# One due time in a fused attention and expert kernel: the turns of a tile are emitted ahead of the next scores

## Chip, cores and metric

The kernel runs on one core of a Trainium2 chip. The time is the device time of one execution in microseconds (us); lower is better. TensorE is called PE, VectorE DVE, ScalarE ACT, GpSimd POOL and SyncE SP, as the profile calls them.

## The reference

Three stages follow each other: attention with a rotation of q and k, a dense layer pair with a gate, and a layer of 8 experts of which each token takes one.

```python
q_rot, k_rot = (rotate(q), rotate(k))            # batch 2, heads 8, seq 576, head_dim 64
scores = scale * np.matmul(q_rot, k_rot.transpose(0, 1, 3, 2))
scores = scores - np.max(scores, axis=-1, keepdims=True)
attn = np.exp(scores)
attn = attn / (np.sum(attn, axis=-1, keepdims=True) + 1e-09)
attn_out = np.matmul(attn, v)
x = attn_out.transpose(0, 2, 1, 3).reshape(B * S, H * D)   # 1152 x 512
h = x @ w_in                                     # 512 x 2048
x = (h * (1.0 / (1.0 + np.exp(-1.702 * h)))) @ w_out
...
expert_idx = np.argmax(x @ w_gate, axis=1)       # 8 experts, at most capacity tokens each
y = np.maximum(disp @ w1, 0.0) @ w2              # per expert, 512 x 1024 x 512
out[i] = gate_w[i] * y[expert_idx[i], pos[i]]
```

## The kernel before, in words

Attention (class `Attention`) goes over 8 pairs p of heads. The queries of a pair stand in 9 tiles i of 128 rows (tile 4 holds the left-over rows of both heads). For each tile:

- `scores(p, i)` (L370) multiplies on PE into a PSUM tile `s` (L393, four matmuls, ten for tile 4), and DVE takes the negated row maximum `nm` from it (L397). `s` has two buffers (pool `ps_s`), so scores i waits until the exponential of scores i-2 has read its buffer.
- `exps(p, i)` (L400) is ACT's exponential of `s` into `pp`, with row sums (L404).
- `turn(p, i)` (L427) transposes the exponentials on PE, four transposes into a PSUM tile `tp` (L442; L434 for tile 4), and copies it to `pt` on ACT or DVE (L212 on ACT, L214 on DVE; the table `SWAPPED` says which).

Around these stand, for each pair: `turn_rest` (tile `tr`, L452), which turns the last 64 columns, and its copies to `ptr`; `turn_sums` (tile `trb`, L472), which turns the reciprocals `rr` of the row sums, and its copy to `tb`; `pv_units` (tile `pv`, L493), the product with v for the two halves a of the pair's tokens, whose last unit multiplies by `tb` on DVE (L496) and writes `xt`; and `qk_units` (tile `tq`, L329), which turns the rotated q and k of the next pair and copies them to `qs` and `ks`. The last q copy is followed by two SP transfers of `qs` into `qx` with the halves exchanged (L344, L345), which the scores of the next pair read. All of `tp`, `tr`, `trb`, `pv` and `tq` come from one PSUM pool of four buffers, `ps_t`.

The order is made in two steps. `run` (L507) gives every unit a due time, one time unit per tile and nine per pair, sorts by it and emits in that order:

```python
at = 9 * p
for i in range(9):
    add(max(at + i - 2 + ORDER["scores"], -1), self.scores, p, i)   # L524
    add(max(at + i - 2 + ORDER["exps"], -1), self.exps, p, i)
    add(at + i + ORDER["turn"], self.turn, p, i)                    # L526
for a in range(2):
    add(at + 4 + 4 * a + ORDER["rest"][a], self.turn_rest, p, a)
    add(at + 4 + 4 * a + ORDER["sums"][a], self.turn_sums, p, a)    # L529
...
    add(at - 9 + ORDER["qk"][k], part, self.qk_units, p, k)         # L536
```

So `scores(p, i+3)` is due at 9p+i+0.174 and `turn(p, i)` at 9p+i+0.191. Then the tile framework, at build time (`TC` at L42 asks it to plan with a model of the machine), lays out the instructions of each engine: among those it holds ready it takes the one emitted first. The order on an engine therefore is not the order of emission: a unit that is not ready is passed by others. On the chip each engine then runs its list in that order.

After attention the class `Experts` computes the dense pair (`first`, `ffn`, `hidden`: L686 and L712), routes the tokens (`route`) and runs the experts (`second`, `few`).

Of the kernel before, what the change touches and what calls it, by code (L numbers as in the profile page):

```python
# [88 lines left out]
WIDE = max(b - a for a, b in zip(CUTS, CUTS[1:])) * TT  # L89
ORDER = {  # L90
    "scores": -0.826,
    "turn": 0.191,
    "exps": 0.692,
    "pv1": (-0.327, 1.359, 1.489, 1.566, 3.949),
    "split": (-0.927, -0.14, 0.12, 2.55),
# [1013 lines left out]
```

## Time and profile before

| What | Value |
|---|---|
| Median of three runs | 508.85 us (507.22 to 508.88) |
| The profiled execution's own time | 510.11 us |
| Its span from the first to the last instruction | 508.3 us |
| PE matmul busy over the span | 469.7 us (92%) |
| DVE, ACT, POOL busy over the span | 366.7 us, 271.6 us, 115.0 us |
| Mean granted TensorE clock | 0.983 |

Busy time is the share of time in which an engine has an instruction under way. Matmuls are pipelined and their ends are modelled, so PE's busy time counts some overlap. A time in brackets behind a row is idle time of the engine ahead of it, with the instruction that ended the wait.

### The profile page before, as it was taken

To read this page: it belongs to the slowest core of one execution; us is meant where nothing else is said; L and a number is where in the kernel's file an instruction comes from. 1 tells how busy PE (TensorE), PEld (TensorE's weight loads), DVE (VectorE), ACT (ScalarE), POOL (GpSimd) and SP (SyncE) were. 2 spreads that over 40 slices of the span, in tenths; PEclk is the share of its full clock that TensorE was granted. 3 is DMA by queue.
4 is the path that set the end of the run, shared out by engine and by line. 5 is a ranking of instruction groups with operands and counts; after the bars stand their busy time and mean duration, and the time that the engine had idled before them with its cause. 6 is when DMAs were issued, how large, how long until landed. Compare 5 with 4: busy or idle time off the path is not lost.

```text
span 508.3 us, 8728 instructions
## 1 busy us (share of the span) xinstructions
PE 469.7 (92%) x3206; PEld 421.6 (83%) x3206; DVE 366.7 (72%) x746; ACT 271.6 (53%) x514; POOL 115.0 (23%) x117
## 2 busy tenths in 40 slices
PE   1789999998999999999999999999999999499992
PEld 1777687687787778788899999999999999499991
DVE  6798999888788998999835534457856689355570
ACT  3577686676565733534563444466566455254640
POOL 5965633422211200000000000000444025601020
PEclk9999999999999999999999999999999999699997
DMA  7032322330224357574101240001076436735410
GB/s 256 1 100 75 99 77 74 99 80 26 53 64 155 105 187 254 188 265 177 41 1 31 63 170 1 0 11 55 2 250 206 132 125 195 246 97 191 162 50 14
DMA packets 20125, 55.63 MB, mean 109 GB/s; under 512 B 3685, under 2 KB 4869, under 8 KB 20080
## 3 DMA queue, kind: packets, MB, share of 16 engines
q1 hardware_dynamic: 17920, 50.91, 31.3%
q0 software_dynamic: 1728, 3.62, 2.4%
q8 instruction: 27, 0.44, 0.4%
q10 hardware_dynamic: 432, 0.51, 0.3%
q14 instruction: 18, 0.15, 0.1%
HBM read 43.86 MB, written 6.66 MB: 99 GB/s over the span
## 4 chain that ended last, share of the span: by engine, by line
PE 61%; DVE 16%; DMA 10%; issue 5%; ACT 4%; POOL 1%; SPq 0%; POOLq 0%; DVEq 0%; ACTq 0%
PE h L686 22%; PE y L712 20%; PE s L393 6%; PE pv L493 4%; DMA qx<-qs 3%; PE tp L442 3%; DVE nm L397 2%; DMA raw<-in_w_out 2%; PE tr L758 2%; DMA raw<-in_w_in 2%; DVE hl L298 2%; ACT pp L404 1%; DVE m L588 1%; DMA got<-x,ent 1%; POOL slots L868 1%
## 5 line engine op out<-in xcount | busy, mean ns | idle before, releaser
L686 PE MATMUL h<-xt,hl 128*128 128x288 f32 (+4 forms) x960 | 175.2, 322 | 1.2 <-DVE hl L673 1.2
L686 PEld LDWEIGHTS h<-xt,hl 128*128 128x128 f32 x960 | 149.0, 191 | 10.2 <-DVE hl L673 2.8
L673 DVE TENSOR_TENSOR hl<-wf,hl 128x1024 fp32r<-128x1024 f32 x80 | 97.5, 1223 | 53.6 <-ACT hl L672 53.4
L712 PE MATMUL y<-gh,hl 128*128 128x288 f32 (+3 forms) x576 | 126.0, 324 | 0.0
L672 ACT ACTIVATE hl<-wf 128x1024 fp32r<-128x1024 f32 x80 | 84.3, 1058 | 52.5 <-PE y L712 25.5
L712 PEld LDWEIGHTS y<-gh,hl 128*128 128x128 f32 x576 | 96.2, 190 | 3.9 <-ACT gh L722 0.4
L712 PE MATMUL y<-gl,hl 128*128 128x288 f32 (+3 forms) x288 | 78.1, 321 | 0.0
L868 POOL DMA_INDIRECT slots<-entry,r_at x12 | 16.5, 1375 | 207.6 <-ACT hl L672 176.8
L397 DVE TENSOR_REDUCE nm<-s 128x1 f32<-128x576 f32 x72 | 53.8, 752 | 12.3 <-PE s L393 10.9
L404 ACT ACTIVATE pp<-s,nm 128x576 f32<-128x576 f32 x64 | 47.7, 745 | 22.7 <-DVE nm L397 22.4
L721 ACT ACTIVATE g<-h 128x480 f32<-128x480 f32 (+2 forms) x48 | 23.5, 492 | 62.6 <-PE h L686 53.2
L393 PE MATMUL s<-ks,qs 128*128 128x288 f32 (+1 forms) x168 | 53.0, 333 | 1.7 <-ACT pp L404 1.3
L712 PEld LDWEIGHTS y<-gl,hl 128*128 128x128 f32 x288 | 51.2, 188 | 1.8
L393 PE MATMUL s<-ks,qx 128*128 128x288 f32 (+1 forms) x168 | 47.0, 306 | 3.4 <-DMA qx<-qs 2.6
L723 DVE TENSOR_TENSOR gl<-g,gh 128x480 fp32r<-128x480 f32 (+2 forms) x48 | 26.5, 554 | 25.1 <-ACT gh L722 24.3
L212 ACT ACTIVATE pt<-tp 128x512 f32<-128x512 f32 x56 | 33.3, 600 | 20.5 <-PE tp L442 20.0
L442 PE MATMUL tp<-ident,pp 128*128 128x128 f32 x256 | 39.8, 281 | 0.5 <-DVE ptr L214 0.5
L493 PE MATMUL pv<-pt,vr 128*64 128x288 f32 x256 | 39.1, 414 | 0.5 <-DVE pt L214 0.3
L393 PEld LDWEIGHTS s<-ks,qs 128*128 128x128 f32 x168 | 32.7, 196 | 7.8 <-issue 3.5
L393 PEld LDWEIGHTS s<-ks,qx 128*128 128x128 f32 x168 | 32.9, 197 | 4.8 <-issue 2.0
L442 PEld LDWEIGHTS tp<-ident,pp 128*128 128x128 f32 x256 | 30.5, 143 | 5.3 <-issue 2.6
L329 PE MATMUL tq<-ident_r,hl 128*128 128x128 f32 x144 | 18.7, 264 | 14.1 <-DVE hl L298 13.5
(178 smaller groups left out, 580.4 us busy)
## 6 DMA issues: line engine op xcount, KB each, us to landing
wf<-in_w SPq DMA_DIRECT2D x32, 512.0 KB, 4.1
raw<-in_w_in SPq DMA_DIRECT2D x16, 512.0 KB, 4.0
raw<-in_w_out SPq DMA_DIRECT2D x16, 512.0 KB, 4.0
qx<-qs SPq DMA_DIRECT2D x14, 320.0 KB, 4.3
qk<-in_qk SPq DMA_DIRECT2D x12, 288.0 KB, 3.2
vr<-in_v SPq DMA_DIRECT2D x8, 320.0 KB, 5.6
x<-row SPq DMA_DIRECT2D x12, 192.0 KB, 2.1
out<-zero SPq DMA_DIRECT2D x9, 256.0 KB, 3.0
```

What stands on the lines that cost most here:

```text
L212: return e.activation(out=out, in_=x, func=AF.Copy, **({} if scale is None else {"scale": scale}))
L393: nc.tensor.matmul(ps[:, n, c:c + w], x, ks[:, src:src + w], start=j == 0, stop=j == len(mine) - 1)
L397: nc.vector.tensor_reduce(out=nm, in_=ps[:, :, 0:HALF], axis=AX.XY, op=ALU.max, negate=True)
L404: nc.scalar.activation(out=out.rearrange("p (n k) -> p n k", n=2), in_=ps[:, :, 0:HALF], func=AF.Exp, bias=d["nm"][:, i:i + 1], accum_out= ...
L442: nc.tensor.transpose(t[:, kt], pp[:, h, h * 64 + kt * P:h * 64 + (kt + 1) * P], self.ident)
L493: nc.tensor.matmul(o[h * 64:h * 64 + 64], x, y, start=j < 2, stop=j > 7)
L672: nc.scalar.activation(out=hl[:, 0], in_=t, func=AF.Copy)
L673: self.last = nc.vector.tensor_tensor(out=hl[:, 1], in0=t, in1=hl[:, 0].bitcast(F32), op=ALU.subtract).ins
L686: self.nc.tensor.matmul(h, u, v, start=m == 0, stop=m == len(ops) - 1)
L712: nc.tensor.matmul(y[j][:, 0:w], u, v, start=f == LAG and m == 0, stop=f == n + LAG - 1 and m == 2)
L721: nc.scalar.activation(out=g, in_=h, func=AF.Gelu_apprx_sigmoid)
L723: nc.vector.tensor_tensor(out=gl, in0=g, in1=gh.bitcast(F32), op=ALU.subtract)
```

## The change

One number in the table of due times is made smaller, so that `turn(p, i)` is due at 9p+i+0.160, ahead of `scores(p, i+3)` at 9p+i+0.174.

```diff
 ORDER = {
     "scores": -0.826,
-    "turn": 0.191,
+    "turn": 0.16,
     "exps": 0.692,
```

Two other units have due times between 0.160 and 0.191 of a step, and the turn now goes ahead of them as well: `turn_sums(p-1, 1)`, due at 9p+0.187, which stood ahead of `turn(p, 0)`; and the first `qk_units` of the next pair (the function `rest` at L350, two transposes and two copies), due at 9p+3.185, which stood ahead of `turn(p, 3)`. No instruction is added or taken away.

## Rows read from the trace of the kernel before

**Rows 1.** Busy time by stretch (PE, PEld, DVE, ACT, POOL; granted clock third from last)

```profile
16.00:185.00 169.00, 161.52 (x1191) 127.76 (x1191) 149.39 (x292) 112.97 (x261) 65.03 (x67) 1.00 0.29 83
...
220.00:300.00 80.00, 79.83 (x423) 73.45 (x422) 52.55 (x93) 37.01 (x54) 0.00 (x0) 1.00 0.29 101
```

**Rows 2.** Waits of PE from 15 to 185 us: total, times, longest

```profile
PE s L393 <- DMA qx<-qs: 2.6, 4, 1.3
```

**Rows 3.** Timeline of PE, first and last turn with the scores behind

```profile
20.52 1.05 PE L442 MATMUL tp<-ident,pp 128*128 128x128 f32 x4
21.23 0.61 PE L393 MATMUL s<-ks,qs 128*128 128x288 f32 x1
...
165.92 0.60 PE L442 MATMUL tp<-ident,pp 128*128 128x128 f32 x4
166.94 0.40 PE L393 MATMUL s<-ks,qs 128*128 128x288 f32 x1 [0.42 <-ACT pp L404]
```

**Rows 4.** Groups of DVE from 15 to 185 us: the turns that DVE copies

```profile
L214 DVE COPY pt<-tp 128x512 f32<-128x512 f32 x16 | 10.8, 677 | 0.0
```

**Rows 5.** Timeline of PE around the start of pair 3

```profile
79.89 0.40 PE L393 MATMUL s<-ks,qs 128*128 128x288 f32 x1 [0.89 <-ACT pp L404]
...
80.62 0.71 PE L493 MATMUL pv<-ptr,vr 128*64 128x288 f32 x4
...
81.25 0.44 PE L472 MATMUL trb<-ident,rr 128*128 128x128 f32 x2
...
81.53 0.60 PE L442 MATMUL tp<-ident,pp 128*128 128x128 f32 x4
```

**Rows 6.** Timeline of PE where pairs 1, 4 and 5 begin

```profile
39.55 0.41 PE L472 MATMUL trb<-ident,rr 128*128 128x128 f32 x2 [0.46 <-DVE rr L214]
...
98.31 0.44 PE L442 MATMUL tp<-ident,pp 128*128 128x128 f32 x2 [0.54 <-DVE ptr L214]
...
119.19 0.44 PE L472 MATMUL trb<-ident,rr 128*128 128x128 f32 x2
119.54 0.40 PE L393 MATMUL s<-ks,qs 128*128 128x288 f32 x1
```

**Rows 7.** Timeline of ACT: the exponential that the last scores of rows 6 wait for

```profile
118.66 0.74 ACT L404 ACTIVATE pp<-s,nm 128x576 f32<-128x576 f32 x1 [3.43 <-DVE nm L397]
```

**Rows 8.** Timeline of PE in pair 2: the next pair's transposes and turn 3

```profile
65.61 0.36 PE L329 MATMUL tq<-ident_r,hl 128*128 128x128 f32 x2
65.81 0.37 PE L393 MATMUL s<-ks,qs 128*128 128x288 f32 x1
...
66.42 0.60 PE L442 MATMUL tp<-ident,pp 128*128 128x128 f32 x4
66.77 0.88 PE L329 MATMUL tq<-ident_r,hl 128*128 128x128 f32 x8
```

**Rows 9.** Timeline of DVE at the same place of pair 1

```profile
46.90 0.28 DVE L214 CAST qs<-tq 128x128 fp32r<-128x128 f32 x1
47.10 0.28 DVE L216 TENSOR_SCALAR ks<-tq 128x128 fp32r<-128x128 f32 x1
47.44 0.76 DVE L397 TENSOR_REDUCE nm<-s 128x1 f32<-128x576 f32 x1
...
49.56 0.71 DVE L397 TENSOR_REDUCE nm<-s 128x1 f32<-128x576 f32 x1
```

**Rows 10.** Timeline of PE: the longest wait for the exchanged q

```profile
115.92 0.37 PE L393 MATMUL s<-ks,qx 128*128 128x288 f32 x1 [1.33 <-DMA qx<-qs]
```

**Rows 11.** Timeline of PE among the experts, ahead of and behind a long wait

```profile
431.73 1.28 PE L686 MATMUL h<-xt,hl 128*128 128x224 f32 x10
...
441.18 0.87 PE L963 MATMUL tg<-ident,got 96*128 96x96 f32 x4 [6.60 <-DMA got<-x,ent]
441.75 2.46 PE L686 MATMUL h<-xt,hl 128*128 128x224 f32 x10
```

**Rows 12.** Busy time by stretch, as rows 1, behind that wait

```profile
442.00:444.00 2.00, 2.00 (x11) 2.00 (x11) 0.56 (x1) 0.49 (x1) 0.00 (x0) 0.50 0.74 213
```

## The prediction

> **What bounds the kernel now.** I first read the busy time by stretch, to see which stage the change can reach. Attention runs to about 185 us, and in its 169 us from 16 us on PE has work under way for 161.5 us, DVE for 149.4 us and ACT for 113.0 us; in the dense pair behind it PE has no gap to speak of, 79.83 of 80 us [rows 1]. So what attention gains or loses is handed on to the end nearly whole, and in attention itself no more than 169 - 161.5 = 7.5 us of PE's idle time could be had. Then I read PE's waits there: the largest that comes back in the loop is the one for the exchanged q, 2.6 us in four places [rows 2]. A step of the change is worth something only if it alters such a wait, or PE's work in front of it.
>
> Then I read PE's timeline unit by unit, and this is the reading that decides. The change swaps turn i and scores i+3 in the order of emission. On PE they already stand in the new order. The first turn runs at 20.52 us and the scores that it is to pass at 21.23 us; the last such turn at 165.92 us and its scores at 166.94 us [rows 3]; counted through all pairs, there are 69 such turns, and in all 69 the turn runs first. The reason can be seen in the code: scores i+3 need the buffer that the exponential of tile i+1 sets free, turn i needs the exponential of tile i only, one exponential earlier. The planner takes what is ready, so the turn never had to compete with these scores. On DVE the copies of the turns could compete with the row maxima; DVE copies 16 turns [rows 4], and each of the 16 stands ahead of the maximum of the scores three tiles on.
>
> **The change, part by part.** Term 1, 69 turns ahead of scores on PE, and 16 copies ahead of maxima on DVE: 0 us. No other work hides it; the order is there already.
>
> Term 2, the first turn of a pair now ahead of the sums' turn (trb) of the pair before, 7 places. The two take tiles from the same pool, and rows 5 show that a later tile of it isn't given out before an earlier one. At 79.89 us the scores of tile 2 of pair 3 start, because the exponential of tile 0 is done; turn 0 needs nothing but that exponential. Still it runs at 81.53 us, behind the last product with v (due 3.8 units later than the turn) and right behind trb [rows 5]. It waited for trb's place, not for data. So I expect trb to move behind turn 0 in all 7 places, about 3 us later in most, and with it trb's copy to tb. Who waits for tb is the multiplication behind the last product with v, which in most pairs itself runs behind turn 0; that product takes 81.25 - 80.62 = 0.63 us [rows 5] and covers the copy, half as wide as a turn's, whose mean is 0.68 us [rows 4]. What the places are worth on PE:
> - Pair 1: trb holds up PE's list for 0.46 us until rr is there [rows 6]. Behind turn 0 it finds rr ready: -0.46 us.
> - Pair 4: turn 0 waits 0.54 us for the buffer that tr leaves [rows 6]; trb had taken an earlier one. In the new order the turn takes that one, and trb may wait in its stead. Between 0 and -0.54 us; I take the middle, -0.25 us, as nothing in the trace shows which buffer falls to which.
> - Pairs 4 and 5: trb filled a hole. In pair 5 it starts at 119.19 us, the scores behind it at 119.54 us [rows 6], and those could not start before the exponential ended at 118.66 + 0.74 = 119.40 us [rows 7]. Taken from there, its 119.54 - 119.19 = 0.35 us comes back as work behind turn 0: +0.35 us, twice, +0.7 us.
> - The other four: trb stands between matmuls that follow without a gap before and after: 0 us.
>
> Term 3, turn 3 now ahead of the first two transposes (tq) for the next pair, 7 places, by the same rule of the pool. Today these two run ahead of scores 5, and turn 3 behind those scores [rows 8]. On PE, 65.81 - 65.61 = 0.20 us moves from in front of scores 5 to behind turn 3; scores 5 start up to 0.20 us earlier, scores 6 as before: 0 us. On DVE their two copies, from 46.90 to 47.44 us, lie in time in which DVE waits for scores 5 anyway [rows 9]. Moved behind that maximum they stand ahead of the maximum of tile 6: 47.44 - 46.90 = 0.54 us more in that stretch, less the 0.20 us by which it starts earlier, 0.34 us. Bounds for 7 pairs: 0 where DVE has a gap there, +2.4 us where every tenth is passed on. In the pair of rows 9 the next maximum starts at 49.56 us as the last of a row of copies, so there DVE has none; but the scores 8 that need this maximum's exponential have some slack of their own in other pairs. I take a third, +0.8 us. The two transfers of qs to qx on SP come behind the last q copy, which ACT or DVE makes after these; nothing else is queued on SP ahead of them. If that copy becomes later, the waits of rows 2 grow by as much; if the planner gives it an earlier place, they shrink. I take 0 us, with bounds of -0.8 us (0.2 us in the four places) and +1.4 us (four times 0.34 us).
>
> Sum: 0 - 0.46 - 0.25 + 0.7 + 0.8 + 0 = +0.8 us. Against the profiled execution's own time of 510.11 us, of which 508.3 us are its span, that is 510.9 us; the median of the runs is 1.26 us below that execution, so on the median 508.85 + 0.8 gives 509.6 us. A measurement of this kernel can tell about 0.5% from no change, 2.5 us, so the band of no change goes from 506.3 to 511.4 us, and this lies inside.
>
> **A rule weighed.** The longest run of nothing but transposes in a pair is that of turn 3 and the eight transposes behind it, twelve [rows 8]; with the two moved in between it is fourteen. In the rows PE holds the granted clock of 1.00, the 2.4 GHz level, through all of attention with those runs of twelve [rows 1]; it stood at 0.50, the 1.2 GHz level, only behind a wait of 6.60 us in which PE did nothing [rows 11, 12]. The Trainium skill, TensorE: Matmul & The Clock Gate, Part 4: PE-mode transpose, says that transposes don't count as activity for the clock as other matmuls do, which speaks against lumping them. The trace doesn't bear it out at twelve. By the rows the term is 0; what it would be by the rule is a rival below.
>
> **The rivals.**
> Slower: the late DVE copies. The mechanism is term 3 without any slack. The two copies go behind the maximum of tile 5; the maximum of tile 6, its exponential, and behind that on ACT the last q copy all come later; the transfer to qx starts later, and PE waits for it at the start of the next pair, as it does for 1.33 us at 115.92 us [rows 10]. Price: the whole 0.54 us [rows 9] in 7 pairs, 3.8 us, with term 2 at -0.46 - 0.25 + 0.7 = 0: 512.6 us. It decides once the maximum of tile 6 comes so late that scores 8 wait for it. For it: DVE's 149.4 of 169 us [rows 1]; against it: the idle time on DVE that the move opens ahead of that maximum.
>
> Faster: the chain through scores 5. If the chain of scores, maximum and exponential decides rather than PE, the 0.20 us that scores 5 gain is kept in 7 pairs, 1.4 us; the two stalls of rows 6 go whole, 0.46 + 0.54 = 1.0 us; and the four waits for q shrink by 0.2 us each, 0.8 us. Together 3.2 us: 505.7 us. For it: PE's busy time holds overlap, since matmul ends are modelled; against it: the work that moves has to run somewhere.
>
> Nothing: if the pool doesn't hold back a later tile and rows 5 have another reason, no instruction moves but perhaps the pair in rows 5: 508.85 us.
>
> The clock: if fourteen transposes let the clock fall, ten matmuls take 2.46 instead of 1.28 us, 0.12 us more for each [rows 11]. With an estimated 20 matmuls until it is back, 2.4 us in each of 7 pairs, 16.5 us: 525 us.
>
> **How the numbers follow.** The forecast near +0.8 us has 0.33, nothing 0.13, both within 0.5%. Slower by the copies has 0.27 and the clock 0.02, faster 0.25. So faster 0.25, same 0.46, slower 0.29. What these prices can't hold is that the planner works from the changed order on: one unit that moves can reorder what follows, in either direction. That is why both outer cases keep a quarter. The likeliest case alone lies between -0.46 - 0.54 + 0.7 - 0.8 = -1.1 us and -0.46 + 0.7 + 2.4 + 1.4 = +4.0 us at its bounds. The range reaches to both outer cases and a little past each: 504.8 to 513.3 us.
>
> **What would show it.** Right, if in the changed kernel trb stands behind turn 0 and the first two tq behind turn 3 in every pair, every turn still ahead of its scores, PE's waits in attention within 1.5 us of today's in sum, and the stall on rr at the start of pair 1 is gone. The slower rival shows as a longer wait for qx at the starts of pairs, with the two small copies between the maxima of tiles 5 and 6. The faster one shows as attention ending some 3 us earlier. If the order on PE is the same as before, the pool doesn't work as I read it. The forecast is wrong if other units, such as products with v or rotations on DVE, change places and a pair's length moves by more than a microsecond.

## The result, and the profile after

| Kernel | Median of its runs | Kernel before, beside it | Ratio, 95% interval |
|---|---|---|---|
| changed kernel | 512.94 us (511.81 to 513.63) | 508.85 us (507.22 to 508.94) | 1.007 (1.005 to 1.0089) |

The change makes the kernel slower by 4.1 us on the medians. That is past the 0.5% that was called no change (506.3 to 511.4 us) and inside the range of 504.8 to 513.3 us. The forecast was 509.6 us.

The profiled execution took 513.63 us, its span 511.7 us. First the busy time by stretch, in the columns of [rows 1]:

```profile
16.00:185.00 169.00, 158.71 (x1179) 126.08 (x1177) 144.87 (x286) 112.57 (x260) 64.23 (x66) 1.00 0.28 79
220.00:300.00 80.00, 79.35 (x417) 72.56 (x416) 54.16 (x96) 36.39 (x53) 0.00 (x0) 1.00 0.31 108
```

From 16 to 185 us PE is busy for 158.71 us, 2.8 us less than in [rows 1], because attention isn't finished there: its last scores start at 169.76 us instead of 166.94 us [rows 3], 2.82 us later. The dense pair behind it is nearly as full as before (79.35 against 79.83 us). So the loss is in attention, and is handed on. Next PE's waits from 15 to 185 us (total, times, longest):

```profile
PE s L393 <- ACT pp L404: 4.8, 5, 2.2
PE s L393 <- DMA qx<-qs: 2.9, 3, 1.1
```

The wait for the exchanged q was 2.6 us [rows 2] and is 2.9 us. What has grown is the wait of scores for an exponential; before it was

```profile
PE s L393 <- ACT pp L404: 1.3, 2, 0.9
```

The longest of these waits stand at the starts of pairs. PE's timeline at the start of pair 3, to be laid beside [rows 5]:

```profile
82.30 0.40 PE L393 MATMUL s<-ks,qs 128*128 128x288 f32 x1 [2.18 <-ACT pp L404]
...
82.95 0.60 PE L442 MATMUL tp<-ident,pp 128*128 128x128 f32 x4
83.38 0.38 PE L472 MATMUL trb<-ident,rr 128*128 128x128 f32 x2
83.69 0.71 PE L493 MATMUL pv<-ptr,vr 128*64 128x288 f32 x4
```

Turn 0 (82.95 us) now runs right behind the scores, and trb (83.38 us) behind it: the order that term 2 foretold, here and at the other six places. But the scores of tile 2 start at 82.30 instead of 79.89 us, behind a wait of 2.18 instead of 0.89 us. The other move shows in pair 2, beside [rows 8]:

```profile
66.78 0.40 PE L393 MATMUL s<-ks,qs 128*128 128x288 f32 x1
...
67.42 0.60 PE L442 MATMUL tp<-ident,pp 128*128 128x128 f32 x4
67.77 1.05 PE L329 MATMUL tq<-ident_r,hl 128*128 128x128 f32 x10
68.66 0.37 PE L393 MATMUL s<-ks,qs 128*128 128x288 f32 x1
...
69.94 0.38 PE L393 MATMUL s<-ks,qs 128*128 128x288 f32 x1
...
70.56 0.46 PE L329 MATMUL tq<-ident_r,hl 128*128 128x128 f32 x4
```

The first two tq stand behind turn 3 as foretold, in one run of ten with the eight that were there. What wasn't foretold is the last row: the four transposes of the second half of q (unit `q_main(1)`, the "last q transposes" below). Before, they ran directly behind tr, ahead of scores 7:

```profile
68.75 0.27 PE L454 MATMUL tr<-ident,prem 128*128 128x128 f32 x1
68.77 0.54 PE L329 MATMUL tq<-ident_r,hl 128*128 128x128 f32 x4
69.15 0.37 PE L393 MATMUL s<-ks,qs 128*128 128x288 f32 x1
```

Now scores 7 (69.94 us) pass them. In pair 2 all four go behind, in pairs 1, 3 and 6 one of the four; in pairs 0, 4 and 5 none, so 7 of the 28 in all. Before, none did in any pair.

### The profile page after: what moved, and what is told of

Its sections match the earlier page's. It is cut to its first block, busy times and chain, and to the rows that moved or that the text cites. A ratio compares the mean times of both kernels' runs of the same rounds, so it can differ in the third digit from the quotient of the medians.

```text
span 511.7 us, 8729 instructions
## 1 busy us (share of the span) xinstructions
PE 469.8 (92%) x3206; PEld 422.4 (83%) x3206; DVE 365.4 (71%) x746; ACT 271.3 (53%) x514; POOL 112.9 (22%) x117
## 4 chain that ended last, share of the span: by engine, by line
PE 63%; DVE 15%; DMA 10%; issue 5%; ACT 4%; POOL 1%; SPq 0%; POOLq 0%; DVEq 0%; ACTq 0%
PE h L686 22%; PE y L712 20%; PE s L393 7%; PE pv L493 4%; PE tp L442 3%; DMA raw<-in_w_in 3%; DMA raw<-in_w_out 2%; PE tr L758 2%; DVE hl L298 2%; DVE nm L397 2%; DVE m L588 1%; ACT pp L404 1%; PE tq L329 1%; DMA qx<-qs 1%; DMA got<-x,ent 1%
## 5 line engine op out<-in xcount | busy, mean ns | idle before, releaser
L397 DVE TENSOR_REDUCE nm<-s 128x1 f32<-128x576 f32 x72 | 53.6, 749 | 11.3 <-PE s L393 11.0
L727 ACT ACTIVATE gh<-h 128x288 fp32r<-128x288 f32 (+2 forms) x32 | 11.5, 358 | 36.5 <-PE h L686 36.4
```

Source lines behind the costliest of these rows:

```text
L397: nc.vector.tensor_reduce(out=nm, in_=ps[:, :, 0:HALF], axis=AX.XY, op=ALU.max, negate=True)
```

## Where the time goes: DVE between two pairs

DVE's timeline where pair 2 ends and pair 3 begins, first of the kernel before, then of the changed one. The last row of each holds the first two maxima of pair 3; the single L397 above it is the maximum of the last scores of pair 2, ahead of which the first timeline begins.

```profile
71.60 0.75 DVE L298 TENSOR_TENSOR hl<-rot,hl 128x576 fp32r<-128x576 f32 x1
...
72.75 0.76 DVE L397 TENSOR_REDUCE nm<-s 128x1 f32<-128x576 f32 x1
73.42 1.03 DVE L298 TENSOR_TENSOR hl<-rot,hl 128x576 fp32r<-128x576 f32 x1
...
75.42 1.02 DVE L416 TENSOR_SCALAR r<-sum 128x4 f32<-128x4 f32 x1
76.35 0.30 DVE L214 CAST xt<-x 128x288 fp32r<-128x288 f32 x1
...
78.16 1.41 DVE L397 TENSOR_REDUCE nm<-s 128x1 f32<-128x576 f32 x2
```

```profile
73.30 0.76 DVE L397 TENSOR_REDUCE nm<-s 128x1 f32<-128x576 f32 x1
73.97 1.42 DVE L298 TENSOR_TENSOR hl<-rot,hl 128x576 fp32r<-128x576 f32 x2
75.31 1.39 DVE L416 TENSOR_SCALAR r<-sum 128x4 f32<-128x4 f32 x1
...
77.09 1.12 DVE L214 CAST xt<-x 128x288 fp32r<-128x288 f32 x1
...
80.58 1.41 DVE L397 TENSOR_REDUCE nm<-s 128x1 f32<-128x576 f32 x2
```

The split of the turned q and k (L298, the lower halves) makes room for the next pair's rotation. Before, one of the two splits began at 71.60 us, ahead of the last maximum. It can only start once the last q transposes have read `hl`, and since these are late, both splits now stand behind that maximum. From there to the first maximum of pair 3 it was 78.16 - 73.42 = 4.74 us and is 80.58 - 73.97 = 6.61 us. Of the 1.87 us, 0.39 us is the splits (1.42 us for the two, where the one took 1.03 us); most of the rest is that the same small instructions take longer, the cast to `xt` 1.12 instead of 0.30 us, r 1.39 instead of 1.02 us. The exponential that the scores at 82.30 us wait for needs that first maximum, and ACT itself stood idle for it:

```profile
81.42 0.74 ACT L404 ACTIVATE pp<-s,nm 128x576 f32<-128x576 f32 x1 [3.77 <-DVE nm L397]
```

This is a reading of one pair, the only one in which all four go late. From the scores of tile 4 in one pair to those of tile 4 in the next, the changed kernel loses 1.54 us there. In pairs 1, 3 and 6 it loses 0.51, 0.38 and 0.21 us, and in pairs 0, 4 and 5, where none goes late, it loses 0.45 us, gains 1.09 us and loses 0.73 us. Whether the late transposes cause a loss, and what makes them late, is what the experiments ask.

## The experiments

**One move at a time.** The two units that the turn passes are moved alone and together, with the turn left at 0.191.

```diff
-    "sums": (1.489, 1.187),
+    "sums": (1.489, 1.2),
```

> One half of the change alone: the sums' turn (trb) goes behind turn 0 of the next pair (its due time 1.187 becomes 1.2), the first tq stays ahead of turn 3. Theory A (the loss sits in the transposes for the next pair, three tq tiles now bunched in the pool of four buffers): 508 to 509.5 us, as before. Theory B (the loss sits in trb and the multiplication by tb at the start of a pair): 512 to 513 us. Theory C (it is the planner's answer to any shift, and not tied to either move): anything, for instance 510 to 512 us here and in the other half too.

Measured: 507.06 us beside 509.01 us, ratio 0.9953 (0.9931 to 0.9975). This move is a gain of 1.95 us, which none of the three theories had: the lowest expectation was 508 us.

```diff
-    "qk": (3.185, 3.985, 4.837, 5.517, 3.808),
+    "qk": (3.195, 3.985, 4.837, 5.517, 3.808),
```

> The other half alone: the first tq goes behind turn 3 (its due time 3.185 becomes 3.195), trb stays ahead of turn 0. Theory A: 512 to 513.5 us, PE's waits for the exponential at the starts of pairs near the 4.8 us of the changed kernel. Theory B: 508 to 509.5 us. Theory C: anything between.

Measured: 512.09 us beside the same 509.01 us, ratio 1.0065 (1.0041 to 1.009): a loss of 3.1 us. Theory A has the time; PE's waits for the exponential are 3.0 us in its profile, not near 4.8 us. Its profiled execution ends attention 5.6 us later than before, and gives part of that back among the experts, where the wait of 6.60 us [rows 11] is 5.0 us. In this kernel the time goes with the granted clock: the five executions with a mean of 0.986 or 0.987 took 509.67 to 511.23 us, the seven with 0.976 to 0.983 took 512.05 to 516.47 us. So a part of the 3.1 us goes with a clock that fell; the last section shows two such falls, both behind stalls at the start of a pair.

Both lines together:

> Both halves, with every turn still due behind the scores (0.191). All theories: the time of the changed kernel, 512 to 513.6 us, since the 55 and more turns that only pass scores should change nothing; if it comes out near 509 us, those turns do count and the reading of the order was wrong.

Measured: 512.95 us, ratio 1.009 (1.0062 to 1.0118); the changed kernel has 512.94 us. The instructions of this kernel stand in the same order on every engine as those of the changed one. So the swap of turns and scores, which gave the change its name, does nothing (term 1), and the two side moves are the whole of it. The loss is in the move of tq. The two do not add: -1.95 and +3.1 make +1.1 us, measured are +3.9 us. On top of the tq move the sums move brings no gain.

**The small copies on ACT.** What makes the last q transposes late? The four buffers of `ps_t` go round in the order of emission, and the last q transposes take the buffer of the k transposes that were emitted four tiles earlier (the first four of the eight at [rows 8]). That buffer is free when its copy is made, for this pair on DVE. (In pairs 0 and 4, where none of the four goes late, ACT makes that copy.) DVE's timeline of the changed kernel:

```profile
67.62 0.76 DVE L397 TENSOR_REDUCE nm<-s 128x1 f32<-128x576 f32 x1 [0.42 <-PE s L393]
68.29 0.28 DVE L214 CAST qs<-tq 128x128 fp32r<-128x128 f32 x1
68.49 0.28 DVE L216 TENSOR_SCALAR ks<-tq 128x128 fp32r<-128x128 f32 x1
...
68.86 0.68 DVE L216 TENSOR_SCALAR ks<-tq 128x512 fp32r<-128x512 f32 x1
...
69.56 0.71 DVE L397 TENSOR_REDUCE nm<-s 128x1 f32<-128x576 f32 x1
```

and of the kernel before:

```profile
66.61 0.76 DVE L397 TENSOR_REDUCE nm<-s 128x1 f32<-128x576 f32 x1
...
67.46 0.68 DVE L216 TENSOR_SCALAR ks<-tq 128x512 fp32r<-128x512 f32 x1
...
68.29 0.76 DVE L397 TENSOR_REDUCE nm<-s 128x1 f32<-128x576 f32 x1
```

The two small copies have moved between the maximum of tile 5 and that k copy, which now starts 0.20 us behind the scores of tile 6 (68.86 - 68.66) where it started 0.03 us ahead of them (67.46 against 67.49). The maximum of tile 6 itself is hardly touched: 0.90 us behind its scores' start instead of 0.80 us. If this is the cause, the tq move must become harmless when ACT makes the two small copies. In pair 1, and likewise in pairs 2 to 7:

```diff
-        "hiq hix1 k0 lok lox0 q0 rest rr1 swapq t5 t7 tb1"
+        "hiq hix1 k0 lok lox0 q0 rr1 swapq t5 t7 tb1"
```

> The kernel before with one thing altered: the two small copies of the first next-pair transposes (q and k of rest) are made by ACT instead of DVE in pairs 1 to 7; no due time is altered. It is the base for the next run. Two theories of the loss of about 3 us (+3.1 us on the median of the run with the qk move alone). Theory D: on DVE these two copies, once moved, stand ahead of the third copy (k of the first half), so the buffer for the last q transposes comes free late, scores 7 pass them, the split of the next q and the rotations after it come late, and at the start of the next pair the first two row maxima wait behind them. Theory E: the lump of ten transposes behind turn 3 costs by itself, whoever copies. Both expect little here: 508 to 511 us, as ACT has idle time at that place but the copies put it ahead of an exponential.

Measured: 509.68 us beside 508.58 us, ratio 1.0014 (0.9995 to 1.0032): alone, the copies on ACT change nothing that is clear of the noise.

> The run rest_act with the qk move added (first tq due 3.195 instead of 3.185). Theory D: the last q transposes stay ahead of scores 7 in all pairs, so the loss goes: within 1 us of rest_act. Theory E: about 3 us slower than rest_act, as with the copies on DVE.

Measured: 509.86 us beside 508.58 us, ratio 1.0027 (1.0008 to 1.0046). The tq move costs 0.2 us with the copies on ACT, where it cost 3.1 us with them on DVE (even the upper end of the interval of rest_act_qk is only 2.3 us above the kernel before); the lump of ten is the same. The last q transposes are back ahead of scores 7 in all pairs; pair 2 in PE's timeline:

```profile
66.66 1.05 PE L329 MATMUL tq<-ident_r,hl 128*128 128x128 f32 x10
...
68.83 0.54 PE L329 MATMUL tq<-ident_r,hl 128*128 128x128 f32 x4
69.21 0.37 PE L393 MATMUL s<-ks,qs 128*128 128x288 f32 x1
```

Theory E, that the lump itself costs, falls. What this pair of runs doesn't separate is the k copy's buffer from DVE's load: with the two copies DVE loses some 0.5 us of work in each pair. The next run leaves the copies on DVE.

**Late transposes without a lump.** The other half of the proof: leave everything of the kernel before in place and make only the last q transposes late.

```diff
-    "qk": (3.185, 3.985, 4.837, 5.517, 3.808),
+    "qk": (3.185, 3.985, 5.2, 5.517, 3.808),
```

> The kernel before with one due time altered: the last q transposes at 5.2 instead of 4.837, so that they go behind scores 7 and turn 5, while the first two tq stay where they were in front of scores 5. Theory D: if lateness of these transposes is what costs, 2 to 6 us slower than before (511 to 515 us), with PE's waits for the exponential at the starts of pairs above 3 us in sum (1.3 us before). Theory E: no lump, so within 1.5 us of before, apart from a longer wait for qx.

Measured: 513.34 us beside 508.58 us, ratio 1.0085 (1.0063 to 1.0106), +4.8 us. PE's wait for the exponential is

```profile
PE s L393 <- ACT pp L404: 5.8, 6, 1.6
```

with the longest at tile 4 of pair 2 (1.60 us), tile 2 of pair 3 (1.45 us) and tile 4 of pair 7 (1.41 us), and DVE's timeline between pairs 2 and 3 is that of the changed kernel, both splits behind the last maximum and the same long r:

```profile
73.00 0.76 DVE L397 TENSOR_REDUCE nm<-s 128x1 f32<-128x576 f32 x1
73.68 1.42 DVE L298 TENSOR_TENSOR hl<-rot,hl 128x576 fp32r<-128x576 f32 x2
75.01 1.38 DVE L416 TENSOR_SCALAR r<-sum 128x4 f32<-128x4 f32 x1
...
80.28 1.41 DVE L397 TENSOR_REDUCE nm<-s 128x1 f32<-128x576 f32 x2
```

So lateness of these transposes costs by itself, without a lump, and the two copies on DVE are what makes some of them late in the changed kernel. The size can't be carried over: here all 28 go behind scores 7, there 7 of them. Here the wait for the exchanged q grew as well, from 2.6 to 3.7 us, so not all of the 4.8 us is DVE's.

**Both moves with the copies on ACT.** The whole effect of the change, with the cause of its loss taken out:

> rest_act_qk with the turn of the sums moved behind turn 0 too (1.2 instead of 1.187): the whole effect of the change, with the two small copies on ACT. Theory D: the gain of the sums move (about 2 us on its own) is kept: 1 to 3 us faster than rest_act. Theory E: 0 to 3 us slower than rest_act.

Measured: 505.91 us beside 508.58 us, ratio 0.994 (0.9918 to 0.9962). This is faster than both kernels, and 3.8 us below rest_act, more than the 1 to 3 us that Theory D gave. To see what each move is worth there, the sums move alone and the pair once more on one chip:

> rest_act with the sums move alone (1.2 instead of 1.187). With rest_act, rest_act_qk and rest_act_both it makes the four cases with the two small copies on ACT. If the two moves simply add there, as Theory D has it once the copies are off DVE (qk move +0.2 us, both -3.8 us against rest_act), this is 4 us faster than rest_act, near 505.7 us. If the sums move is worth what it was with the copies on DVE, 1.9 us, it is near 507.8 us, and the qk move itself then gains 2 us beside it.

Measured: 507.46 us beside 508.82 us, ratio 0.9982 (0.9961 to 1.0003).

> The kernel of rest_act_both once more, on the chip of rest_act_sums, so that the two are compared with the same runs of the kernel before. It stood 2.7 us below before; 2 to 3.5 us below is expected again.

Measured: 505.98 us beside 508.82 us, ratio 0.9947 (0.993 to 0.9965). With the copies on ACT the four cases stand, against the kernel before on their own chip, at +1.1 us (none), +1.3 us (tq), -1.4 us (sums) and -2.7 and -2.8 us (both). By the medians they don't add here either: beside the sums move the tq move gains about 1.4 us, without it it loses 0.2 us. My expectation of 505.7 us for the sums move alone was off, and the second case that I had written down for it, 507.8 us, was near. Why the moves help each other here and hinder each other with the copies on DVE is left open.

How far single positions can be trusted: the two profiled executions of this last kernel, the same list of instructions, end attention 2.1 us apart, and PE's wait for the exchanged q is 1.6 us in one and 3.8 us in the other. Until the end of pair 4 they agree within 0.3 us; they part at the start of pair 5, where one waits 1.2 us for the exchanged q and the other doesn't. The medians are the evidence for the sizes above; single places serve to show what happens.

## Why the forecast missed

**What bounds the kernel** was read rightly: attention is the stage that the change reaches, and what it loses there (2.8 us of PE's timeline) comes out at the end. Most of the loss went into PE's waits, as said there. That the time lies inside the range is the range's doing, which reached to the slower rival, and not that of the sum.

**Term 1, 0 us: right.** All 69 turns still run ahead of their scores, and the kernel in which only the two side units move has the order and the time of the changed one.

**Term 2, order right, size wrong.** trb went behind turn 0 in all seven places. The sum -0.46 - 0.25 + 0.7 = 0 measured -1.95 us. The +0.7 us of pairs 4 and 5, where trb, taken out of its hole, should come back as work, held at pair 5 alone. In PE's timeline of sums_only the scores of tile 4 start 0.28 us (pair 1), 0.42, 0.37, 0.83, 0.59, 1.18 and 1.42 us (pair 7) ahead of the kernel before. The step at pair 4 is a gain of 0.46 us, that at pair 5 a loss of 0.24 us, near its 0.35 us, and at pairs 6 and 7, which I had at nothing, 0.59 and 0.24 us are gained; these are positions of one execution. The stalls on rr at pair 1 and on the buffer of tr at pair 4 went as foretold; for the latter trb waits 0.2 us in the turn's stead. I took a unit that fills a hole as free, and asked only what its work costs elsewhere; the time at which turn 0 and everything behind it come free earlier was not in the sum.

**Term 3 is the step that failed.** "I take a third, +0.8 us" charged the two late copies to the maximum of tile 6 alone. Counted from the scores of tile 4, that maximum came at most 0.23 us later in any pair. What I left out is the third copy in DVE's list, the k copy, whose buffer the last q transposes need. I did write that the last q copy could become later, and looked for the price at its transfers, "the waits of rows 2 grow by as much"; in sum these went from 2.6 to 2.9 us only. Where the price can be followed, between pairs 2 and 3, it was paid one link on: transposes late, `hl` free late, split late, and DVE's list ahead of the first maxima of the next pair longer. In numbers, +0.8 us stands against +3.1 us for the move alone. How the rest of that divides among the pairs stays open.

**The sum itself failed too.** It added the terms as if neither altered the other. With the measured -1.95 and +3.1 us it would have come to +1.1 us, and the change to about 510 us; the 2.8 us that are missing to the measured +3.9 us of the two moves are in no term.

**The slower rival** had the right unit (two copies on DVE) and the right sign. That its price is near (512.6 us, measured 512.94 us) is luck: it was made of +3.8 and 0 us, and the two moves measured +3.1 and -1.95 us alone and +3.9 us together. Its place was right in part. Its sign, a longer wait for qx at the starts of pairs, is hidden in the sum: the waits were 0.80, 1.33, 0.16 and 0.31 us at pairs 1, 5, 6 and 7, and are 1.09, 0, 1.07 and 0.77 us, so three of them grew by 1.66 us together and the longest, that of [rows 10], is gone. ACT's timeline of pair 4 shows what went with that, first before, then changed:

```profile
108.05 0.78 ACT L404 ACTIVATE pp<-s,nm 128x576 f32<-128x576 f32 x1
...
108.77 0.64 ACT L212 ACTIVATE qs<-tq 128x512 fp32r<-128x512 f32 x1
```

```profile
111.12 0.60 ACT L212 ACTIVATE qs<-tq 128x512 fp32r<-128x512 f32 x1
111.61 0.74 ACT L404 ACTIVATE pp<-s,nm 128x576 f32<-128x576 f32 x1
```

The last q copy now stands ahead of the exponential of tile 6, 0.61 us sooner after the scores of tile 4, and its transfer starts sooner. So the planner did both things that term 3 named, an earlier place here and a later one elsewhere. Scores 8, which need that exponential, start 0.4 us later in pairs 4 and 5, where ACT's order changed in this way. In pair 1 they start 0.5 us later; there the q copy stands ahead of the exponential in both kernels, and is itself 0.56 us later behind the late transpose.

**The other rivals.** The faster one fits one of the two moves: the sums move alone gains 1.95 us, though without the 0.20 us of scores 5, which belonged to the tq move. Nothing falls, as the pool works as read. The clock: the run of ten transposes with four more ahead of it held the granted clock at 1.00 in the profiled execution of the changed kernel, so that rival falls as it was put. Its 20 matmuls until the clock is back come from no row of the kernel before; where the clock fell in attention (last section), twelve or thirteen matmuls ran at the lower level in some 3 us.

Of the signs that were to show it, the two orders, the turns and the stall on rr came out right. "PE's waits within 1.5 us of today's" came out wrong, and was the sign of the loss: 4.8 us against 1.3 us on the exponentials alone. The last sign, rotations on DVE that change places and a pair's length that moves by more than a microsecond, came true: between pairs 2 and 3 the rotation's sum (L280) went from 74.38 us, ahead of r, to 78.13 us, behind the cast, and that stretch grew by 1.54 us.

Not settled: why the wait for the exchanged q grew at pairs 1 and 6, ahead of which no transpose was late (the second transfer took 5.9 us from issue to landing there, 4.3 to 4.5 us for the other pairs); and why the sums move adds nothing once the tq move is in with the copies on DVE.

## What to carry to other kernels

When a change passes a unit, don't stop at the next instruction behind its copies. Follow the list of the copying engine to the first copy that frees a buffer, from there to the work that takes that buffer, and on to what that work frees; where the price could be followed here, it was paid two links on, half a pair later. A swap that the data already forces is worth nothing, so count first what else lies in the interval that a due time crosses, and try each of these alone and together, for their effects need not add: one of the two gained 1.95 us and the other lost 3.1 us, and moving two small copies to another engine turned the whole from +4.1 to -2.7 us.

## What the runs showed of the hardware

**DVE behind POOL.** The r at L416 is a tiny TENSOR_SCALAR. Its 16 places in the changed kernel up to 185 us (shortest, median and longest in ns; then first and last start):

```profile
L416 DVE TENSOR_SCALAR r<-sum x16: 157/160/1393, 28.5 to 174.5; 128x5 f32<-128x5 f32 x8, 128x4 f32<-128x4 f32 x8
```

It takes 0.16 us, and in two places 1.39 us. In both, POOL was at a rotation when it began; in the kernel before there are five such places, all of over 1 us, four of them beside a rotation and one beside a split on POOL. It ends with POOL's instruction, to some hundredths: before, the r at 75.42 us ends at 76.44 us, and in POOL's timeline

```profile
74.54 1.87 POOL L276 TENSOR_TENSOR rot<-qk,turns 128x576 f32<-128x576 f32 x1 [0.69 <-DVE hl L298]
```

ends at 76.41 us. The Trainium skill, SBUF — State Buffer, Who interferes with whom, says that a tensor_scalar on DVE can run in a mode that contends with GpSimd for a shared pair of ports, and that the one that issues second is then blocked until the first is done. The rows agree: the price of the small instruction is what is left of the large one. In sum the changed kernel has fewer of these long r than before, so they alone are not its loss. Between pairs 2 and 3 they are part of it: the late splits let go two rotations of POOL one right behind the other,

```profile
74.80 3.24 POOL L276 TENSOR_TENSOR rot<-qk,turns 128x576 f32<-128x576 f32 x2 [8.71 <-DVE hl L298]
```

and r and the cast to `xt`, which began beside them, take 1.19 us longer together, of the 1.87 us. So the same small work between two pairs can take 1 us more or less, depending on when POOL's rotation is let go. No run here took POOL's rotation away, so its share of the 1.87 us was not measured by itself.

**The clock at a stalled pair start.** The list of instructions of both_moves is that of the changed kernel. Its profiled execution has the same wait at the start of pair 3:

```profile
82.16 0.40 PE L393 MATMUL s<-ks,qs 128*128 128x288 f32 x1 [2.19 <-ACT pp L404]
```

and behind it, in the busy time by stretch (granted clock third from last),

```profile
83.00:86.00 3.00, 3.00 (x13) 1.81 (x12) 2.06 (x4) 1.32 (x3) 0.34 (x1) 0.51 0.02 5
```

PE runs at 1.2 GHz there. The changed kernel's own execution, with 2.18 us of the same wait, kept 2.4 GHz:

```profile
80.00:88.00 8.00, 5.82 (x43) 4.82 (x42) 6.99 (x12) 5.01 (x12) 2.91 (x4) 1.00 0.29 96
```

In the profiled execution of qk_only it fell at the starts of pairs 1 and 3:

```profile
42.00:44.00 2.00, 2.00 (x10) 1.10 (x10) 0.00 (x0) 1.24 (x3) 1.86 (x3) 0.50 0.00 0
...
86.00:88.00 2.00, 2.00 (x9) 1.98 (x10) 1.50 (x3) 0.45 (x2) 0.91 (x2) 0.50 0.47 133
```

Ahead of the first of these PE had stood still for 0.81 and 0.45 us between 37 and 40 us, ahead of the second for 1.80 us up to 83.77 us. At the lower level the four transposes of a turn took 1.11 us (at 41.61 us), where they take 0.60 us [rows 5]. So waits of a microsecond or two in sum at the start of a pair can cost twice, in one execution and not in the next; in the kernel before the granted clock is 1.00 all through attention [rows 1].
